# Block-sparse attention and soft mixture of experts: scores of two query blocks in one pass over the array

## The chip, the cores and the metric

The kernel runs on one core of one Trainium2 chip. The core has a matrix engine (TensorE, here PE, whose loads of stationary operands are listed as PEld), VectorE (DVE), ScalarE (ACT), GpSimd (POOL) and a queue engine (SP) that issues transfers. The metric is the device time of one execution in microseconds; the median of the runs counts. All data are float32.

## The reference, cut to what matters

```python
# B, H, S, D = 4, 8, 768, 64; blocks of 32 tokens, 24 blocks
scores = scale * np.matmul(q, k.transpose(0, 1, 3, 2))
mask = np.abs(blk_i - blk_j) <= 1                       # window of three blocks
mask = mask | (blk_i == 0) | (blk_j == 0) | (blk_i == n_blocks - 1) | (blk_j == n_blocks - 1)
for qb in range(n_blocks):
    for kb in sampled_blocks[qb]:                       # three drawn blocks per query block
        mask[qb*32:(qb+1)*32, kb*32:(kb+1)*32] = True
attn = softmax(np.where(mask, scores, -1e9));  x = attn @ v      # x: 3072 tokens, 512 wide
logits = x @ phi                                        # 32 slots: 8 experts, 4 slots each
slot_input = softmax(logits, over tokens).T @ x
slot_out[e] = relu(slot_input[e] @ w1[e]) @ w2[e]       # w1: 512 x 1024, w2: 1024 x 512
out = softmax(logits, over slots) @ slot_out
```

So the first and the last query block see all 768 keys ("dense"), and each of the 22 others sees at most 256: the two global blocks, its window of three, and three drawn blocks.

## The kernel before

**Units.** The attention is a list of 104 units, 26 per batch. A dense unit holds two heads of query blocks 0 and 23; there are four per batch. A sparse unit is one query block i (1 to 22) with all eight heads. Heads are stored in pairs: the transposed keys of a pair lie on 128 partitions, 64 for each head (`ktile`, four pairs of 768 columns, one batch at a time).

**Stages of a sparse unit.** `stage_k` gathers 256 key columns for the four pairs into one of `NKST` buffers `kst`: GpSimd copies the global and the window blocks (lines 190, 193), ScalarE the three drawn ones (line 199), whose numbers it loads into registers. `stage_v` loads the matching rows of V into one of eight buffers `vst`: SP issues the global and window rows, GpSimd an indirect gather of 96 rows (line 219). `do_qk` computes scores with four matmuls (line 306): the stationary operand holds, for one pair of heads, 64 columns, two heads of 32 queries, and each head's column is zero on the other head's 64 partitions; the 256 staged keys are the moving operand. Pairs 0 and 2 write partitions 0 to 63 and pairs 1 and 3 partitions 64 to 127 of one PSUM tile `s` of 128 by 2 by 256. `do_soft` takes the row maximum on VectorE (`nm`, line 322) and the exponential on ScalarE (`p`, line 325). `do_tr` transposes the 128 by 512 probabilities in four pieces on PE (`ps`, line 354) and copies them to SBUF (`ptt`), one unit on ScalarE (line 335), the next on VectorE (line 337). Four units make a tile of 128 tokens; `av_half` then multiplies by V for heads 0 to 3 and for heads 4 to 7 (`av`, line 391, 32 matmuls each), V's last column being ones for the sum, and VectorE divides (lines 398 to 400).

**Stages of a dense unit.** The same steps under the names `sd` (line 298), `nm`, `pd`, `psd` (line 345, six transposes in two banks), `ptd` and `avd` (line 371).

**Behind each tile** run the steps of `moe_front`: transposes of the tokens (`mxt`), logits (`mlp`, `mlt`), their running maximum and exponential (`nmx`, `dT`), a transpose (`md`) and the sum into the slot input (`ms`, `sacc`). `EOFF` says how many half steps after the tile each comes.

**Order.** PE and VectorE execute in the order in which the code is written: the loop at line 585 calls, for unit n, the scores of unit n+2 (line 589), what is due first (`X1`), the transposes of unit n, and what is due second (`X2`). ScalarE, GpSimd and SP get their order from a scheduler. SP issues nearly all transfers in one queue: queries (`qc`, three buffers), V, keys of the next batch, and pieces of the expert weights, `NPRE` of which are loaded during the attention.

**PSUM** has eight banks: the tag "s" (`SB` of them, scores), "pt" (`TB`, everything transposed or of `moe_front`) and "av" (two). A tile of a tag waits until the tile that last used that bank has been read.

**The experts** follow: `pf` (line 714) and `pso` (line 722) read each weight once, with 32-column stationary operands on four column strips, and `po` (line 814) combines.

Of the kernel before, what the change touches and what calls it, by code (L numbers as in the profile page):

```python
# [11 lines left out]
F32 = mybir.dt.float32  # L12
# [9 lines left out]
P = 128  # L22
# [3 lines left out]
NE, SE, FF = 8, 4, 1024  # L26
NT = S // P
# [17 lines left out]
# experts: w2 in CS column parts, weights in pieces of WP, NPRE of them loaded during the attention  # L45
# [7 lines left out]
NPRE, NLA, NLB = 29, 3, 12  # L53
# [9 lines left out]
def attn_moe_kernel(ctx, tc, qT, kT, vtab, sampled, phi, w1, w2, out):  # L63
# [9 lines left out]
    # the weights come in pieces of [P, WP]  # L73
# [75 lines left out]
    # ================= attention =================  # L149
# [7 lines left out]
    # but for the first, in the order in which the end of the attention frees them, the last first  # L157
# [3 lines left out]
    qc = [pst.tile([P, NP, 2, 2 * BLK], F32, name=f"qc{n}") for n in range(NQ)]  # L161
# [7 lines left out]
    def load_q(b, c):  # L169
        SP.dma_start(out=qc[(b * (NB // 2) + c) % NQ], in_=qT[b, c])  # L170

    def q_of(b, i):
        c = (i + 1) // 2
        return qc[(b * (NB // 2) + c) % NQ][:, :, (i + 1) % 2, :]
# [60 lines left out]

    class U:
        pass

    # the tokens go in tiles of four blocks: (1, 2, 0, 23), (3 .. 6), ... (19 .. 22)
# [26 lines left out]
    def do_stage(u):  # L266
        if u.dense:
            if u.pair == 0 and u.b:
                load_q(u.b, 0)
                load_k(u.b)  # L270
                load_q(u.b, 1)
# [634 lines left out]
```

## Time and profile before

| | us |
|---|---|
| median of 3 runs | 395.05 (394.22 to 395.6) |
| span of the profiled execution, first to last instruction | 410.4 |
| attention within it, about | 13 to 347 |
| PE busy | 353.6 |
| DVE, ACT, POOL busy | 220.0, 209.9, 142.3 |

The profiled execution has no other time than its span, which is 15.4 us above the median; its rows are used for durations and shares. Its mean granted clock of PE is 0.963. Several rows of a product stand for one matmul: a float32 matmul makes two records, a transpose one. A group of the profile is written `line engine operation out<-in shapes xcount | busy us, mean ns of one | idle before it, and what ended that idle time`.

### The profile page before, as it was taken

The numbers are of one execution on the slowest core, as the hardware profiler recorded it, in microseconds if no ns is written. First come the engines' busy times: TensorE is split into PE (matmuls) and PEld (weight loads), VectorE is DVE, ScalarE is ACT, GpSimd is POOL, SyncE is SP. The second block draws the span as 40 slices with busy tenths as digits, with TensorE's granted clock in tenths as the row PEclk, the third lists the DMA queues.
The fourth block names the chain that finished last, engine by engine and source line by source line (L and its number), as shares of the span: only waits on it lengthen the run. The fifth ranks groups of instructions, "written<-read, shape, count | busy, mean of one in ns | idle before, by whom it ended". The sixth has DMA issues, their size and how long they took to land.

```text
span 410.4 us, 14102 instructions
## 1 busy us (share of the span) xinstructions
PE 353.6 (86%) x5525; PEld 228.1 (56%) x5525; DVE 220.0 (54%) x618; ACT 209.9 (51%) x689; POOL 142.3 (35%) x216
## 2 busy tenths in 40 slices
PE   5788988799899867998999698989989899799970
PEld 2456655467566544665665465657556556435550
DVE  3655635466455535676565356756556687501350
ACT  1655756466457625672766276638556563310350
POOL 1625425432153544234445244333453243120000
PEclk9999999899899989999999799999999899999995
DMA  7977999989859979999599759965965499899978
GB/s 242 299 221 224 312 291 246 287 272 314 214 153 286 264 237 312 292 274 286 140 271 274 244 164 277 309 173 147 265 162 138 124 242 396 308 357 410 360 248 250
DMA packets 47841, 105.56 MB, mean 257 GB/s; under 512 B 6976, under 2 KB 13856, under 8 KB 47776
## 3 DMA queue, kind: packets, MB, share of 16 engines
q1 hardware_dynamic: 42144, 87.08, 68.5%
q0 software_dynamic: 5632, 17.58, 16.4%
q8 instruction: 44, 0.72, 0.8%
q14 instruction: 21, 0.17, 0.1%
HBM read 98.34 MB, written 6.29 MB: 255 GB/s over the span
## 4 chain that ended last, share of the span: by engine, by line
PE 81%; issue 6%; DVE 3%; DMA 3%; SPq 2%; ACT 1%; POOL 1%; ACTq 0%; POOLq 0%; DVEq 0%
PE s L306 22%; PE av L391 13%; PE ps L354 12%; PE sd L298 6%; PE pso L722 4%; PE pf L714 3%; PE mxt L413 3%; PE avd L371 3%; PE psd L345 3%; PE mlt L465 2%; PE ms L497 2%; PE mlp L458 2%; DMA ktile<-in_kT_dram 2%; PE po L814 2%; DMA vst<-in_vtab_dram 1%
## 5 line engine op out<-in xcount | busy, mean ns | idle before, releaser
L219 POOL DMA_INDIRECT vst<-in_vtab_dram,gidx x88 | 83.3, 946 | 111.9 <-PE av L391 89.2
L306 PE MATMUL s<-kst,qc 128*64 128x256 f32 x704 | 100.8, 404 | 8.9 <-issue 6.3
L199 ACT ACTIVATE kst<-ktile 128x128 f32 x264 | 67.0, 312 | 56.7 <-PE ps L354 18.9
L322 DVE TENSOR_REDUCE nm<-s 128x2 f32<-128x512 f32 x88 | 60.4, 687 | 45.5 <-PE s L306 20.4
L325 ACT ACTIVATE p<-s,nm 128x256 f32<-128x256 f32 x176 | 73.9, 475 | 12.0 <-DVE nm L322 9.6
L193 POOL TENSOR_SCALAR kst<-ktile 128x384 f32<-128x384 f32 x88 | 45.3, 519 | 76.0 <-PE s L306 62.2
L391 PE MATMUL av<-vst,ptt 128*32 128x65 f32 x2816 | 59.2, 225 | 12.0 <-issue 10.9
L306 PEld LDWEIGHTS s<-kst,qc 128*64 128x64 f32 x704 | 44.7, 139 | 38.0 <-issue 19.2
L391 PEld LDWEIGHTS av<-vst,ptt 128*32 128x32 f32 x2816 | 49.2, 111 | 20.4 <-issue 17.9
L354 PE MATMUL ps<-ident,p 128*128 128x128 f32 x352 | 58.9, 291 | 0.0
L354 PEld LDWEIGHTS ps<-ident,p 128*128 128x128 f32 x352 | 38.0, 143 | 22.1 <-issue 14.0
L337 DVE COPY ptt<-ps 128x512 f32<-128x512 f32 x44 | 30.2, 685 | 34.2 <-PE av L391 22.0
L335 ACT COPY ptt<-ps 128x512 f32<-128x512 f32 x44 | 25.8, 587 | 40.3 <-PE ps L354 26.2
L319 ACT ACTIVATE pd<-sd,nb 128x384 f32<-128x384 f32 x32 | 17.7, 579 | 32.0 <-DVE nb L316 17.1
L298 PE MATMUL sd<-ktile,qc 128*128 128x384 f32 x64 | 27.9, 564 | 5.1 <-DMA ktile<-in_kT_dram 5.1
L400 DVE TENSOR_TENSOR x<-av,rs 128x256 f32<-128x256 f32 (+1 forms) x48 | 20.3, 423 | 1.6
L313 DVE TENSOR_REDUCE nm<-sd 128x1 f32<-128x384 f32 x32 | 17.1, 553 | 7.2 <-PE sd L298 4.8
L337 DVE COPY xT<-mxt 128x512 f32<-128x512 f32 (+2 forms) x25 | 16.5, 661 | 7.4 <-PE mxt L413 3.5
L345 PE MATMUL psd<-ident,pd 128*128 128x128 f32 x96 | 14.8, 293 | 5.3 <-DVE ptt L337 5.3
L298 PEld LDWEIGHTS sd<-ktile,qc 128*128 128x128 f32 x64 | 12.3, 215 | 12.4 <-DMA qc<-in_qT_dram 4.3
L371 PEld LDWEIGHTS avd<-vst,ptd 128*64 128x64 f32 x384 | 13.7, 143 | 7.0 <-DVE ptd L337 2.1
L497 PE MATMUL ms<-x,d 128*32 128x128 f32 x192 | 10.2, 285 | 8.3 <-DVE ptt L337 7.1
(110 smaller groups left out, 352.4 us busy)
## 6 DMA issues: line engine op xcount, KB each, us to landing
w<-in_w_dram SPq DMA_DIRECT2D x64, 512.0 KB
vst<-in_vtab_dram SPq DMA_DIRECT2D x80, 195.0 KB
qc<-in_qT_dram SPq DMA_DIRECT2D x47, 256.0 KB
vst<-in_vtab_dram SPq DMA_DIRECT2D x24, 260.0 KB
ktile<-in_kT_dram SPq DMA_DIRECT2D x15, 384.0 KB
out_dram<-ob SPq DMA_DIRECT2D x20, 256.0 KB
vst<-in_vtab_dram SPq DMA_DIRECT2D x72, 65.0 KB
vst<-in_vtab_dram,gidx POOLq DMA_INDIRECT x88
```

What stands on the lines that cost most here:

```text
L193: POOL.tensor_scalar(out=st[:, :, BLK:P], in0=kv[:, :, (i - 1) * BLK:(i + 2) * BLK], scalar1=SCALE, scalar2=1.0, op0=ALU.mult, op1=ALU.mult)
L199: ACT.activation(out=st[:, :, 160 + BLK * j:192 + BLK * j], in_=kv[:, :, ds(vals[j] * BLK, BLK)], func=AF.Copy, scale=SCALE)
L219: POOL.indirect_dma_start(out=st[32:128, 1, :], out_offset=None, in_=vflat, in_offset=bass.IndirectOffsetOnAxis(ap=gidx[:, b, i:i + 1], ax ...
L298: PE.matmul(u.s[n], lhsT=qc[u.b * (NB // 2) % NQ][:, u.pair].rearrange("p a c -> p (a c)"), rhs=ktile[:, u.pair, 384 * n:384 * (n + 1)], s ...
L306: PE.matmul(u.s[64 * c:64 * c + 64, hf, :], lhsT=q[:, p, :], rhs=u.kst[:, p, :], start=True, stop=True)
L322: DVE.tensor_reduce(out=nm, in_=u.s, axis=AX.X, op=ALU.max, negate=True)
L325: ACT.activation(out=u.p[:, hf, :], in_=u.s[:, hf, :], func=AF.Exp, bias=nm[:, hf:hf + 1], scale=1.0)
L337: DVE.tensor_copy(out=out, in_=in_)
L345: PE.transpose(ps[:, k, :], u.p[g][:, k * P:(k + 1) * P], ident)
L354: PE.transpose(ps[:, 2 * hf + k, :], u.p[:, hf, k * P:(k + 1) * P], ident)
L371: PE.matmul(a[64 * h2:64 * h2 + 64, u.pair, :], lhsT=u.pt[k][:, 64 * h2:64 * h2 + 64], rhs=vd[u.b][k][:, h * 65:h * 65 + 65], start=(k == ...
L391: PE.matmul(a[32 * c:32 * c + 32, hh, :], lhsT=u.pt[:, 2 * hf + k, hh * 32:hh * 32 + 32], rhs=u.vst[:, k, h * 65:h * 65 + 65], start=(k == ...
```

## The change

One score pass now serves two query blocks, a "pair" of units with blocks 2g+1 and 2g+2. Heads are paired as (p, p+4): the first four heads lie on partitions 0 to 63, the last four on 64 to 127. A score matmul takes one head of one block: a stationary operand of 64 partitions by 32 columns, without zeros, and the 64 partitions of `kst` that hold this head. Head p of the first four goes to partitions 32p of one PSUM tile, head p+4 to the same partitions of a second tile. So unit r of a pair no longer holds one block with eight heads but both blocks with four heads; its tile is again 128 by 2 by 256, the middle index being the block. Maximum, exponential, transposes and copies keep their sizes and their count. `av_half` for heads 4r to 4r+3 now follows unit r of the tile's second pair. It has 32 matmuls as before.

With it change: query transfers (`qT` without zeros, 128 KB per pair; the dense blocks' zero-padded queries apart, `qd`, 256 KB per batch), `NKST` 3 to 4, `SB` 3 to 4, `TB` 3 to 2, `NPRE` 29 to 28, the order of a batch's first units, the last of `EOFF`, and the end of the last tile. Comments were removed too; they are left out here.

```diff
+NG2 = NB // 2 - 1
-NKST, NV, NQ = 3, 8, 3
+NKST, NV, NQ = 4, 8, 3
-SB, TB = 3, 3
+SB, TB = 4, 2
-ORDER0 = "DDSDDSS"
-ORDER = "DSDDDSS"
+ORDER0 = "DDSSDDSS"
+ORDER = "DSSDDDSS"
-EOFF = [3, 6, 8, 9, 11, 15]
+EOFF = [3, 6, 8, 9, 11, 14]
-NPRE, NLA, NLB = 29, 3, 12
+NPRE, NLA, NLB = 28, 3, 12
...
-    qc = [pst.tile([P, NP, 2, 2 * BLK], F32, name=f"qc{n}") for n in range(NQ)]
+    qd = pst.tile([P, NP, P], F32, name="qd")
+    qc = [pst.tile([P, NP, 2, BLK], F32, name=f"qc{n}") for n in range(NQ)]
...
-        for i in range(1, NB - 1):
-            u = U()
-            u.b, u.i, u.dense = b, i, False
-            sparse.append(u)
+        for g in range(NG2):
+            us = [U(), U()]
+            for r, u in enumerate(us):
+                u.b, u.g, u.r, u.dense, u.pair_of = b, g, r, False, us
+                u.i = 2 * g + 1 + r
+            sparse += us
...
-        if u.i % 2 == 0 and u.i // 2 + 1 < NB // 2:
-            load_q(u.b, u.i // 2 + 1)
+        if u.r == 1 and u.g + 1 < NG2:
+            load_q(u.b, u.g + 1)
         u.kst = stage_k(u.b, u.i)
...
-        else:
-            q = q_of(u.b, u.i)
-            u.s = psA.tile([P, 2, 256], F32, tag="s", name="s", bufs=SB)
-            for hf in range(2):
-                for c in range(2):
-                    p = 2 * hf + c
-                    PE.matmul(u.s[64 * c:64 * c + 64, hf, :], lhsT=q[:, p, :],
-                              rhs=u.kst[:, p, :], start=True, stop=True)
+        elif u.r == 0:
+            q = qc[(u.b * NG2 + u.g) % NQ]
+            for v in u.pair_of:
+                v.s = psA.tile([P, 2, 256], F32, tag="s", name="s", bufs=SB)
+            for j in range(2):
+                kst_ = u.pair_of[j].kst
+                for p in range(NP):
+                    for r in range(2):
+                        s_ = slice(64 * r, 64 * r + 64)
+                        PE.matmul(u.pair_of[r].s[32 * p:32 * p + 32, j, :], lhsT=q[s_, p, j, :],
+                                  rhs=kst_[s_, p, :], start=True, stop=True)
...
             for k in range(2):
                 for u in us:
-                    c = quad(u.i)
-                    PE.matmul(a[32 * c:32 * c + 32, hh, :], lhsT=u.pt[:, 2 * hf + k, hh * 32:hh * 32 + 32],
-                              rhs=u.vst[:, k, h * 65:h * 65 + 65], start=(k == 0), stop=(k == 1))
+                    for j in range(2):
+                        c = quad(2 * u.g + 1 + j)
+                        PE.matmul(a[32 * c:32 * c + 32, hh, :], lhsT=u.pt[:, 2 * j + k, hh * 32:hh * 32 + 32],
+                                  rhs=u.pair_of[j].vst[:, k, h * 65:h * 65 + 65], start=(k == 0), stop=(k == 1))
...
-                t = (u.i + 1) // 4
-                bytile.setdefault((u.b, t), []).append(u)
-                if u.i % 4 == 2:
-                    us = bytile.pop((u.b, t))
+                t = (u.g + 1) // 2
+                bytile.setdefault((u.b, t, u.r), []).append(u)
+                if u.g % 2 == 0:
+                    us = bytile.pop((u.b, t, u.r))
+                    go = lambda b=u.b, t=t, us=us, hf=u.r: av_half(b, t, us, hf)
                     if n == N - 1:
-                        last = [lambda hf=hf, us=us: av_half(B - 1, NT - 1, us, hf) for hf in range(2)]
+                        last = go
                     else:
-                        for hf, X in ((0, X1), (1, X2)):
-                            X.setdefault(n + 1, []).append(lambda b=u.b, t=t, us=us, hf=hf: av_half(b, t, us, hf))
+                        X1.setdefault(n + 1, []).append(go)
...
-    last[0]()
-    one()
     one()
     e = moe_front(B - 1, NT - 1)
-    last[1]()
+    last()
+    one()
...
-    kt = k.reshape(B, NP, 2, S, D).transpose(0, 1, 2, 4, 3).reshape(B, NP, 2 * D, S)
+    kt = k.reshape(B, 2, NP, S, D).transpose(0, 2, 1, 4, 3).reshape(B, NP, 2 * D, S)
```

How the order on the engines moves. First PE in the middle of a batch, between two groups of av matmuls (rows: line, operation, out<-in, size of the output, count). Before:

```order
L306 MATMUL s<-kst_91,qc_102 64x256 x4
L354 MATMUL ps<-ident,p 128x128 x4
L482 MATMUL md<-ident,dT 128x32
L413 MATMUL mxt<-ident,x 128x128 x4
L306 MATMUL s<-kst_100,qc_103 64x256 x4
L354 MATMUL ps<-ident,p 128x128 x4
L306 MATMUL s<-kst_101,qc_103 64x256 x4
L458 MATMUL mlp<-xT,phis 32x128 x4
L354 MATMUL ps<-ident,p 128x128 x4
L497 MATMUL ms<-x,d 32x128 x4
```

And now:

```order
L359 MATMUL ps<-ident,p 128x128 x8
L489 MATMUL md<-ident,dT 128x32
L420 MATMUL mxt<-ident,x 128x128 x4
L311 MATMUL s<-kst_91,qc_104 32x256 x8
L311 MATMUL s<-kst_100,qc_104 32x256 x8
L359 MATMUL ps<-ident,p 128x128 x4
L504 MATMUL ms<-x,d 32x128 x4
L465 MATMUL mlp<-xT,phis 32x128 x4
```

The transposes of two units now stand next to each other with md and mxt behind them, all in the "pt" banks; ms stands ahead of mlp. VectorE at the same place, now, from the copy of the first of those two units on:

```order
L342 COPY ptt<-ps 128x512
L327 TENSOR_REDUCE nm<-s 128x2
L342 COPY d<-md 128x32
L493 SCALAR_TENSOR_TENSOR ssum<-ssum,al,sm 128x1
L342 COPY xT<-mxt 128x512
L327 TENSOR_REDUCE nm<-s 128x2
L342 COPY ptt<-ps 128x512
L327 TENSOR_REDUCE nm<-s 128x2
L507 SCALAR_TENSOR_TENSOR sacc<-sacc,al,ms 128x128
```

The copy of the third transposed unit stands behind the reduction of scores that PE computes just ahead of that unit's transposes, as it did before. In the dense units (PE), before:

```order
L345 MATMUL psd<-ident,pd 128x128 x6
L497 MATMUL ms<-x,d 32x128 x4
L306 MATMUL s<-kst_91,qc_104 64x256 x4
L465 MATMUL mlt<-lp,sel_69 128x128
L466 MATMUL mlt<-sel_69,lp 128x32
L371 MATMUL avd<-vst_94,ptd 64x65 x4
```

And now:

```order
L376 MATMUL avd<-vst_94,ptd 64x65 x4
L350 MATMUL psd<-ident,pd 128x128 x6
L376 MATMUL avd<-vst_99,ptd 64x65 x4
L376 MATMUL avd<-vst_95,ptd 64x65 x4
L376 MATMUL avd<-vst_94,ptd 64x65 x4
L350 MATMUL psd<-ident,pd 128x128 x6
```

One of the four groups of transposes psd has no score product between it and the avd that uses it.

More of the change, by code (lines that the diff above doesn't have):

```diff
@@ L62, in attn_moe_kernel @@
 @with_exitstack
-def attn_moe_kernel(ctx, tc, qT, kT, vtab, sampled, phi, w1, w2, out):
+def attn_moe_kernel(ctx, tc, qD, qT, kT, vtab, sampled, phi, w1, w2, out):
     nc = tc.nc
@@ L167, in load_k, with load_q @@
             SP.dma_start(out=ktile[:, p, :], in_=kT[b, p])
[L169 to L174, printed above, removed]
+    def load_q(b, g):
+        SP.dma_start(out=qc[(b * NG2 + g) % NQ], in_=qT[b, g])
     nsp = [0]
@@ L268, in do_stage @@
             if u.pair == 0 and u.b:
+                SP.dma_start(out=qd, in_=qD[u.b])
+                load_k(u.b)
                 load_q(u.b, 0)
[L270 to L271 removed]
             return
[L273 to L274 removed]
+        if u.r == 1 and u.g + 1 < NG2:
+            load_q(u.b, u.g + 1)
         u.kst = stage_k(u.b, u.i)
@@ L297, in do_qk @@
             for n in range(2):
-                PE.matmul(u.s[n], lhsT=qc[u.b * (NB // 2) % NQ][:, u.pair].rearrange("p a c -> p (a c)"),
-                          rhs=ktile[:, u.pair, 384 * n:384 * (n + 1)], start=True, stop=True)
-        else:
-            q = q_of(u.b, u.i)
-            u.s = psA.tile([P, 2, 256], F32, tag="s", name="s", bufs=SB)
-            for hf in range(2):
-                for c in range(2):
-                    p = 2 * hf + c
-                    PE.matmul(u.s[64 * c:64 * c + 64, hf, :], lhsT=q[:, p, :],
-                              rhs=u.kst[:, p, :], start=True, stop=True)
+                PE.matmul(u.s[n], lhsT=qd[:, u.pair], rhs=ktile[:, u.pair, 384 * n:384 * (n + 1)], start=True, stop=True)
+        elif u.r == 0:
[9 more added lines that the diff above has]
+                                  rhs=kst_[s_, p, :], start=True, stop=True)
     def do_soft(u):
@@ L369, in av_dense @@
             for h2 in range(2):
-                h = 2 * u.pair + h2
+                h = u.pair + 4 * h2
                 PE.matmul(a[64 * h2:64 * h2 + 64, u.pair, :], lhsT=u.pt[k][:, 64 * h2:64 * h2 + 64],
```

32 lines of the change are left out of this document (16 added, 16 removed).

## The prediction

> **What bounds the kernel now.** I read the page first, then the chain of waits, then the table by stretches.
>
> ```profile
> span 410.4 us, 14102 instructions
> PE 353.6 (86%) x5525; PEld 228.1 (56%) x5525; DVE 220.0 (54%) x618; ACT 209.9 (51%) x689; POOL 142.3 (35%) x216
> PE 81%; issue 6%; DVE 3%; DMA 3%; SPq 2%; ACT 1%; POOL 1%; ACTq 0%; POOLq 0%; DVEq 0%
> ```
>
> TensorE (PE) carries 81% of the chain that ends last. The attention lasts from about 13 to 347 us. The rows of the table by stretches, for all of it and for two groups of four sparse units (a tile of tokens), give busy time of PE, PEld, DVE, ACT, POOL, then the granted clock, DMA share and GB/s:
>
> ```profile
> 13.00:347.00 334.00, 300.08 (x4978) 199.74 (x4978) 196.55 (x544) 191.24 (x645) 133.73 (x190) 0.97 0.85 244
> 129.75:142.11 12.36, 10.91 (x205) 7.19 (x209) 6.87 (x19) 7.19 (x26) 5.78 (x9) 1.00 1.00 285
> 297.84:310.00 12.16, 10.73 (x206) 7.04 (x209) 6.87 (x19) 6.99 (x26) 5.79 (x9) 1.00 0.68 175
> ```
>
> PE is busy in 300 of 334 us. The two tiles take nearly the same time although the DMA share is 1.00 in one and 0.68 in the other, so transfers do not set the pace. The chain through the second tile, in order of time (start, length, what):
>
> ```profile
> 297.84 1.17 PE av L391 x64
> 299.01 0.59 PE ps L354 x4
> 299.60 1.04 PE av L391 x64
> 300.65 1.01 PE s L306 x8
> 301.66 0.59 PE ps L354 x4
> 302.25 0.18 PE md L482
> 302.43 0.59 PE mxt L413 x4
> 303.01 1.01 PE s L306 x8
> 304.03 0.59 PE ps L354 x4
> 304.61 1.01 PE s L306 x8
> 305.63 0.35 PE mlp L458 x8
> 305.98 0.65 PE ps L354 x4
> ...
> 306.65 0.69 DVE nm L322
> 307.35 0.61 DVE ptt L337
> ...
> 308.00 0.43 PE ms L497 x8
> 308.42 1.01 PE s L306 x8
> ```
>
> Two things are to be seen. Scores (s) are four pieces of 1.01 us, a third of the tile. And between 306.63 and 308.00 PE waits 1.37 us: ms needs a bank of the "pt" rotation that the copy ptt empties, and that copy stands behind a reduction in VectorE's (DVE's) order. This is the only stall of the tile.
>
> **The scores: what is saved.** A unit's four matmuls are eight records (two passes each) in 1.01 us; 88 units make 88.9 us. What is a record worth? These pieces of the chain are a full-width product of 384 columns, and second-layer expert products of 256 columns on quarters of the array:
>
> ```profile
> 99.17 1.49 PE sd L298 x4
> 374.85 6.61 PE pso L722 x120
> ```
>
> A full-width record takes 1.49/4 = 0.372 us, scaled to 256 columns 0.248. A score record now takes 1.01/8 = 0.126, so a group of two (both column halves) lasts 0.253. An expert record takes 6.61/120 = 0.055, a group of four (all column quarters) 0.220. So a group lasts 0.22 to 0.25 us whatever the number of column strips that share it. The new pair of units has 16 matmuls, 32 records, in four groups of eight (four strips, two row halves). No row of the trace has two row halves at work together; I bound it. If all eight run together: 4 x 0.253 = 1.01 us (4 x 0.220 = 0.88 at best). If the row halves follow each other: 8 x 0.253 = 2.02. I take 1.01, since strips in the other direction share with no loss in the rows above, and the two halves write different banks. Saved: 44 pairs x (2.02 - 1.01) = 44.4 us; bounds 50 and 0. The other arithmetic is unchanged: as many reductions, exponentials, transposes and av matmuls.
>
> The Trainium skill, "TensorE: Matmul & The Clock Gate", Part 3, section "Measured speedup vs the span model", speaks against full sharing: four row tiles gave 3.07x and nine tiles 6.32x. An estimate from that page for eight tiles is 5.6x. On the 0.497 us that a 256-column matmul takes alone (two records of 0.248) 16 matmuls would then take 1.42 us a pair, and the saving would be 26 us. The trace disagrees for columns: four strips give 0.248/0.055 = 4.5x.
>
> **What is given back: the banks.** The "pt" rotation (ps, psd, mxt, mlp, mlt, md, ms) falls from three banks to two, because two units' scores now need two banks at once. What frees a bank:
>
> ```profile
> L322 DVE TENSOR_REDUCE nm<-s 128x2 f32<-128x512 f32 x88 | 60.4, 687 | 45.5 <-PE s L306 20.4 <-PE ps L354 18.4 <-ACT p L325 2.8
> L337 DVE COPY ptt<-ps 128x512 f32<-128x512 f32 x44 | 30.2, 685 | 34.2 <-PE av L391 22.0 <-PE sd L298 10.1 <-PE ps L354 1.3
> L335 ACT COPY ptt<-ps 128x512 f32<-128x512 f32 x44 | 25.8, 587 | 40.3 <-PE ps L354 26.2 <-PE s L306 8.4 <-issue 5.6
> L400 DVE TENSOR_TENSOR x<-av,rs 128x256 f32<-128x256 f32 x40 | 17.0, 424 | 1.3
> L199 ACT ACTIVATE kst<-ktile 128x128 f32 x264 | 67.0, 312 | 56.7 <-PE ps L354 18.9 <-issue 13.0 <-PE s L306 11.8
> ```
>
> In the new order PE does av, ps, ps, md, mxt, s (two units), ps, ms, mlp. Let av end at 0. The ps end at 0.59 and 1.18. DVE first does what av released (the multiplication alone 0.42, two small operations before it, together about 0.75), then the copy of the first ps, 0.685: md, which takes that bank, starts at 1.48 instead of 1.18, 0.30 late. mxt needs ScalarE's (ACT's) copy of the second ps, 1.18 + 0.04 + 0.587 = 1.81, against 1.66 at which md ends: 0.15 late; ACT has up to six key copies (0.312 each, overlapping) ahead of such a copy in its order, and I add 0.2. The scores then end at 3.6, the third ps 0.59 later; its copy stands behind the reduction of those scores: 3.6 + 0.04 + 0.69 + 0.685 = 5.0, while mlp, which takes that bank, would start at 3.6 + 0.59 + 0.43 = 4.6: 0.4 late. Together about 1.1 us per tile, 24.2 us for 22 tiles. Bounds: nothing, if the copies are early, and 2 us per tile, if ACT's are twice as late as worked out. Against that stands what the trace already pays, in the waits of PE:
>
> ```profile
> PE av L391 <- issue: 10.9, 8, 3.3
> PE ms L497 <- DVE ptt L337: 7.1, 5, 1.9
> PE s L306 <- issue: 6.3, 4, 2.5
> ```
>
> The 7.1 us go: ms now takes mxt's bank, emptied during the scores. Net +17.1.
>
> **Smaller terms.** In the dense units each group of six transposes psd had a score product (1.01) behind it before avd; now once per batch avd follows at once and waits for both copies, about 0.6 us, 4 x 0.6 = +2.5 (bounds 0 and 5). PE's instruction records grow from 2 x 5525 by 2 x 704, 13%; if the "issue" stalls in front of av and s (10.9 + 6.3) are late instructions, they grow by 13%: +2.3 (0 to 5). Then transfers:
>
> ```profile
> 350.00:372.00 22.00, 20.54 (x205) 8.91 (x209) 5.99 (x28) 4.44 (x12) 4.04 (x7) 1.00 0.90 339
> w<-in_w_dram SPq DMA_DIRECT2D x64, 512.0 KB
> qc<-in_qT_dram SPq DMA_DIRECT2D x47, 256.0 KB
> ```
>
> One weight piece of 512 KB less is loaded ahead; at 339 GB/s that is +1.5 us in the expert stage, where the DMA share is 0.90 (nothing, if PE there hides it). Queries fall from 47 issues of 256 KB to 44 of 128 KB and four of 256 KB; they are issued ahead on SP's queue and hidden by PE work, so I count 0, and the lower traffic covers the shorter stage. Without that cover, 0.85 x 334 = 284 us of DMA work would still fit into the new 313. The fourth key stage lets ACT and GpSimd run further ahead, which both halves of the pair need: 0.
>
> Sum: -44.4 + 17.1 + 2.5 + 2.3 + 1.5 = -21.0. The profiled span would go from 410.4 to 389.4. The profiled execution is 15 us above the median of 395.05; I take the difference over unchanged: **374 us**.
>
> **Rivals.** (1) The waits do not come: copies are early enough, the 7.1 goes and the small terms stay: -44.4 - 7.1 + 6.3 = -45, 350 us. For it: DVE is busy in 6.87 of 12.16 us; against it: the order on DVE, by which the third copy cannot precede the reduction. (2) Half of the sharing is lost: 1.5 us per pair, saved 22.9, given back 23.4: 395 us, no change. For it: the bound between 1.01 and 2.02 is open; against it: column strips lose nothing. The page named above would land near here. (3) The change does not do what it says: row halves follow each other, a pair costs 1.76 to 2.02 (8 x 0.220 or 0.253), 0 to 11 us saved, 23.4 given back: 407 to 418 us, slower. (4) The two banks decide: every transposed block waits for a copy queued behind others on DVE or ACT; from 2.0 us per tile on, 22 tiles eat the 44 us; at 2.4 us it is -44.4 + 52.8 - 7.1 + 6.3 = +7.6, 403 us. For it: the one stall that the tile shows is of this kind and is already 1.37 us with three banks; against it: my chain gives half.
>
> **How the numbers follow.** Chances: forecast 0.60 (its own range 363 to 385, by 0.6 to 1.6 us of waits per tile), rival 1 0.12, rival 2 0.10, rival 3 0.10, rival 4 0.08. A measurement can tell about 0.3% from no change. Faster by more: 0.60 + 0.12 + 0.04 of rival 2 = 0.76; within: 0.04; slower: 0.10 + 0.08 + 0.02 = 0.20. The range from 355 to 402 leaves out rival 3 and part of rivals 1 and 4, under 0.2.
>
> **What would show it.** In the changed profile the score line should show 1408 records, and a pair in the chain 0.9 to 1.1 us for 32 records; 1.8 or more means rival 3, about 1.5 rival 2. In a tile, md, mxt and mlp should follow waits for ptt of 0.2 to 0.5 us each, and ms none. A tile as free of other stalls as the quoted one should take 12.16 - 2.02 - 1.37 + 1.1 = 9.9 us. The forecast is wrong if waits of PE for ptt sum to over 45 us, or if the pair is not near 1 us.

## The result: 5% slower, and the profile after

The changed kernel takes 413.3 us (median), the kernel before, beside it on the same chip, 394.6 us. The ratio is 1.053, with an interval from 1.045 to 1.061. The forecast was 374 us, the stated range 355 to 402. Ratios leave out executions over 1.5% longer than the fastest of the same kernel, here and below, so they can differ by up to about 1% from those of the medians beside them.

The page of the changed kernel has these rows for the span, the busy times and the chain of waits:

```profile
span 410.8 us, 15471 instructions
PE 322.8 (79%) x6229; PEld 215.3 (52%) x6229; DVE 222.6 (54%) x618; ACT 212.8 (52%) x689; POOL 141.9 (35%) x220
PE 52%; DVE 13%; ACT 11%; DMA 11%; issue 6%; ACTq 2%; SPq 1%; DVEq 0%
```

PE carried 81% of the chain before; now it carries 52%, and VectorE (DVE), ScalarE (ACT) and transfers carry 35%. The group of scores, before and now (busy, mean of one, idle before it and who ended it):

```profile
L306 PE MATMUL s<-kst,qc 128*64 128x256 f32 x704 | 100.8, 404 | 8.9 <-issue 6.3
L311 PE MATMUL s<-kst,qc 64*32 64x256 f32 x1408 | 55.0, 413 | 6.4 <-ACT kst L198 2.9
```

The scores fell from 100.8 to 55.0 us of PE, so what the change is about came in full: 45.8 us. What came with it is seen best in one tile. First a tile of the kernel before (stretch, length, busy time of PE, PEld, DVE, ACT, POOL, clock, DMA share, GB/s), then the tile at the same place in the change and a second tile of the change, with a few more records:

```profile
292.11:302.42 10.31, 10.31 (x196) 6.89 (x195) 6.28 (x16) 7.42 (x28) 3.71 (x7) 1.00 0.61 160
```

```profile
295.83:306.43 10.60, 8.81 (x226) 6.17 (x226) 6.57 (x17) 8.14 (x29) 4.72 (x7) 1.00 0.62 175
223.29:234.31 11.02, 9.01 (x234) 6.42 (x234) 6.92 (x18) 7.70 (x28) 5.75 (x9) 1.00 0.60 163
```

Before, an undisturbed tile was PE work without a gap, 10.31 of 10.31 us. Now PE works 8.81 us of 10.60: 1.5 us of work are gone, and 1.8 us of waiting have taken their place. The chain through the second one, from one mxt to the next (start, length, what):

```profile
223.29 0.66 PE mxt L420 x4
223.94 1.14 PE s L311 x32
225.08 0.67 DVE nm L327
225.75 0.61 DVE ptt L342
226.36 0.04 issue
226.40 0.43 PE mlp L465 x8
226.83 1.31 PE av L398 x64
228.14 0.59 PE ps L359 x4
228.73 1.02 PE s L311 x32
...
231.29 0.29 ACT kst L198
231.59 0.72 ACT p L330 x2
232.31 0.35 ACT dT L480 x2
232.66 0.18 ACT al L484
232.85 0.08 ACT lst L485
232.93 0.04 issue
232.97 0.67 PE ps L359 x4
233.64 0.02 issue
233.67 0.59 ACT ptt L340
234.26 0.04 issue
234.31 0.65 PE mxt L420 x4
```

The pair of scores takes 1.02 to 1.14 us. Three times the chain leaves PE: ahead of mlp for the copy ptt behind the reduction nm (1.3 us), ahead of ps for lst (1.7 us), and ahead of mxt for ScalarE's ptt (0.65 us). PE has a little other work meanwhile and idles 11.02 - 9.01 = 2.0 us of these 3.7. The second is the largest: ps needs the bank that mlt holds until ScalarE has read it for dT and lst, and ScalarE has key copies and two exponentials ahead of these. Over the whole kernel, PE's longest waits are these (total, times, longest); that of the last row lies at the start of the kernel and was there before (5.1 us):

```profile
PE ps L359 <- ACT lst L485: 18.5, 12, 4.9
PE av L398 <- issue: 13.7, 6, 4.3
PE mxt L420 <- ACT ptt L340: 5.8, 12, 0.5
PE mlp L465 <- DVE ptt L342: 5.5, 12, 1.0
PE sd L301 <- DMA ktile<-in_kT_dram: 5.5, 2, 4.3
```

The batch changes got longer as well. The two intervals between tiles around a batch change sum to 31.0, 30.0 and 31.0 us, against 23.6, 23.4 and 24.6 in the kernel before. The chain at the second one, and the table for two stretches there:

```profile
165.00 9.52 DMA ktile<-in_kT_dram
...
177.24 0.08 ACT lst L485
177.32 0.04 issue
177.37 1.13 PE ps L359 x4
```

```profile
165.00:174.60 9.60, 5.75 (x190) 4.22 (x189) 3.94 (x11) 2.43 (x7) 0.22 (x1) 1.00 0.87 256
174.60:180.00 5.40, 2.58 (x13) 1.88 (x12) 2.22 (x7) 4.43 (x19) 4.40 (x9) 0.54 0.87 287
```

The next batch's keys land late, ScalarE's copies of them stand ahead of p, dT, al and lst of the old batch, and PE waits 2.4 us for lst. When it goes on its granted clock is 0.54: four transposes take 1.13 instead of 0.59 us. But the lower clock begins at 175.0, when this wait has just begun. Ahead of it lies another wait, with no cause in the profile (start, length, what, idle before):

```profile
173.73 0.66 PE L398 MATMUL av<-vst,ptt 128*32 128x65 f32 x32 [3.36 <-issue]
```

The Trainium skill ("TensorE: Matmul & The Clock Gate", "What's actually happening") says that the clock falls to half after at least one idle window of about 3.4 us. The trace agrees here, with 3.36 us and 0.54; elsewhere in it half the clock also follows shorter waits (2.7 us, at 89.2).

**The account.** PE outside the scores was busy 353.6 - 100.8 = 252.8 us and is now 322.8 - 55.0 = 267.8: 15.0 us more for the same arithmetic. The clock, 0.963 before and 0.917 now, makes 252.8 x 0.963 / 0.917 = 265.5 of it, that is 12.7 of the 15.0 us. The span outside PE's busy time is 410.8 - 322.8 = 88.0 us. For the kernel before it would be about 394.6 - 1.8 - 353.6 = 39.2 us, an estimate, since its profiled execution was longer than the timed ones; it takes PE's busy time to be the same in both. So -45.8 (scores) + 15.0 (slower PE) + 48.8 (waits) = +18.0.

### The profile page after: what moved, and what is told of

It is laid out like the page before. It is cut to its first block, busy times and chain, and to the rows that moved or that the text cites. A ratio compares the mean times of both kernels' runs of the same rounds, so it can differ in the third digit from the quotient of the medians.

```text
span 410.8 us, 15471 instructions
## 1 busy us (share of the span) xinstructions
PE 322.8 (79%) x6229; PEld 215.3 (52%) x6229; DVE 222.6 (54%) x618; ACT 212.8 (52%) x689; POOL 141.9 (35%) x220
## 3 DMA queue, kind: packets, MB, share of 16 engines
q0 software_dynamic: 5632, 17.58, 16.1%
## 4 chain that ended last, share of the span: by engine, by line
PE 52%; DVE 13%; ACT 11%; DMA 11%; issue 6%; ACTq 2%; SPq 1%; DVEq 0%
DMA ktile<-in_kT_dram 10%; PE s L311 9%; PE av L398 8%; PE ps L359 6%; PE sd L301 5%; PE pf L720 4%; DVE ptt L342 4%; PE mxt L420 4%; PE pso L728 4%; DVE nm L327 3%; PE avd L376 3%; ACT kst L198 3%; PE psd L350 3%; ACT ptt L340 2%; ACT p L330 2%
## 5 line engine op out<-in xcount | busy, mean ns | idle before, releaser
L198 ACT ACTIVATE kst<-ktile 128x128 f32 x264 | 63.8, 302 | 46.5 <-DMA ktile<-in_kT_dram 13.7
L330 ACT ACTIVATE p<-s,nm 128x256 f32<-128x256 f32 x176 | 73.3, 471 | 17.4 <-DVE nm L327 16.7
L398 PE MATMUL av<-vst,ptt 128*32 128x65 f32 x2816 | 61.0, 224 | 17.6 <-issue 13.7
L398 PEld LDWEIGHTS av<-vst,ptt 128*32 128x32 f32 x2816 | 52.5, 111 | 24.5 <-issue 16.6
L359 PEld LDWEIGHTS ps<-ident,p 128*128 128x128 f32 x352 | 41.6, 152 | 42.1 <-ACT lst L485 21.4
L311 PE MATMUL s<-kst,qc 64*32 64x256 f32 x1408 | 55.0, 413 | 6.4 <-ACT kst L198 2.9
L311 PEld LDWEIGHTS s<-kst,qc 64*32 64x32 f32 x1408 | 23.1, 112 | 23.2 <-issue 13.2
L301 PE MATMUL sd<-ktile,qd 128*128 128x384 f32 x64 | 28.2, 571 | 5.5 <-DMA ktile<-in_kT_dram 5.5
L405 DVE TENSOR_SCALAR rs<-av 128x4 f32<-128x4 f32 (+1 forms) x48 | 7.6, 159 | 42.2 <-PE av L398 41.7
L420 PE MATMUL mxt<-ident,x 128*128 128x128 f32 x92 | 17.8, 325 | 11.0 <-ACT ptt L340 5.8
L342 DVE COPY xT<-mxt 128x512 f32<-128x512 f32 (+2 forms) x25 | 16.6, 664 | 17.6 <-PE mxt L420 17.2
L301 PEld LDWEIGHTS sd<-ktile,qd 128*128 128x128 f32 x64 | 13.0, 226 | 12.2 <-issue 4.8
L189 POOL TENSOR_SCALAR kst<-ktile 128x256 f32<-128x256 f32 x16 | 6.4, 397 | 37.0 <-DMA ktile<-in_kT_dram 28.6
```

What stands on the lines that cost most here:

```text
L198: ACT.activation(out=st[:, :, 160 + BLK * j:192 + BLK * j], in_=kv[:, :, ds(vals[j] * BLK, BLK)], func=AF.Copy, scale=SCALE)
L301: PE.matmul(u.s[n], lhsT=qd[:, u.pair], rhs=ktile[:, u.pair, 384 * n:384 * (n + 1)], start=True, stop=True)
L311: PE.matmul(u.pair_of[r].s[32 * p:32 * p + 32, j, :], lhsT=q[s_, p, j, :], rhs=kst_[s_, p, :], start=True, stop=True)
L330: ACT.activation(out=u.p[:, hf, :], in_=u.s[:, hf, :], func=AF.Exp, bias=nm[:, hf:hf + 1], scale=1.0)
L342: DVE.tensor_copy(out=out, in_=in_)
L359: PE.transpose(ps[:, 2 * hf + k, :], u.p[:, hf, k * P:(k + 1) * P], ident)
```

## The experiments

They ran in five sets, each on a chip of its own, and the kernel before was timed beside each set. On the third chip it took 391.7 us, much as on the chip of the result; on the other four 414 to 416 us, where all kernels are slower (the last section says how). So only kernels of one set are compared in us, others by their ratio.

| kernel | us | before beside it | ratio (interval) |
|---|---|---|---|
| b0: the kernel before, profiled again | 419.0 | 414.6 | one run |
| one_key_load | 440.0 | 414.6 | 1.068 (1.062 to 1.074) |
| two_key_tiles | 441.1 | 414.6 | 1.070 (1.064 to 1.077) |
| three_banks | 432.9 | 414.6 | 1.048 (1.043 to 1.054) |
| change_again | 446.3 | 413.7 | 1.080 (1.073 to 1.088) |
| before_two_banks | 446.5 | 413.7 | 1.077 (1.068 to 1.086) |
| act_as_written | 432.1 | 413.7 | 1.045 (1.036 to 1.054) |
| two_key_tiles_act_as_written | 434.5 | 413.7 | 1.047 (1.039 to 1.055) |
| scores_twice | 467.7 | 391.7 | 1.193 (1.183 to 1.204) |
| one_av_bank | 403.6 | 391.7 | 1.032 (1.023 to 1.040) |
| one_av_bank_act_as_written | 378.6 | 391.7 | 0.963 (0.952 to 0.973) |
| three_banks_act_as_written | 393.6 | 391.7 | 1.006 (1.001 to 1.011) |
| before_act_as_written | 435.5 | 416.1 | 1.054 (1.037 to 1.070) |
| before_one_av_bank_act_as_written | 449.9 | 416.1 | 1.083 (1.059 to 1.106) |
| dense_first | 446.2 | 416.1 | 1.085 (1.075 to 1.094) |
| one_av_bank_act_as_written_two_key_tiles | 422.4 | 416.1 | 1.026 (1.016 to 1.035) |
| fastest_again | 417.5 | 414.9 | 1.000 (0.995 to 1.005) |
| old_scores_again | 447.6 | 414.9 | 1.068 (two executions, no interval) |

The theories: (1) the keys' reload is exposed by its place in SP's queue; (2) by the single key tile; (3) two banks for what is transposed cost more than the scores save; (4) ScalarE's scheduled order holds PE up.

### The kernel before once more

No edit. 

> The kernel before, profiled again, since its first profiled execution (span 410.4 us) was some 15 us longer than its timed runs. If the difference lay in that one execution's late instructions (PE waited 17.2 us with nothing to wait for in front of av and s), this span is 393 to 397 us, those waits are under 5 us, and tiles take 10.3 to 10.5 us throughout. If the profiler itself costs 15 us on this kernel, the span is about 410 again.

It took 419.0 us with a span of 417.2. This chip is one of the slow kind, so the run did not give the undisturbed trace it was meant for. The waits without a visible cause were as in the first profile (16.1 us in front of av and s, 17.2 there); they are not an accident of one execution.

### The keys

```diff
-        for p in range(NP):
-            SP.dma_start(out=ktile[:, p, :], in_=kT[b, p])
+        SP.dma_start(out=ktile, in_=kT[b].rearrange("p d s -> d p s"))
```

> The change, with the next batch's keys loaded by one transfer of 1.5 MB in place of four, so that SP cannot put five loads of V between the first part and the other three (in the changed kernel's trace these go out 3.6 us apart: part 1 at 160.5, parts 2 to 4 at 164.06). Theory 1 (the keys' reload is exposed because of its place on SP's queue): each of three batch changes gets about 3.5 us shorter, 402 us. Theory 2 (it is exposed because there is one key tile, and the place does not matter): no change, 411 to 414 us. Theory 3 (banks and ScalarE's order alone made the change slow): no change either.

```diff
-    ktile = pk.tile([P, NP, S], F32, name="ktile")
+    ktiles = [pk.tile([P, NP, S], F32, name=f"ktile{n}") for n in range(2)]
...
-NPRE, NLA, NLB = 28, 3, 12
+NPRE, NLA, NLB = 25, 3, 12
```

> The change, with two key tiles in turn instead of one, and 25 weight pieces loaded ahead instead of 28 (three pieces of 512 KB are worth at most 4.6 us in the expert stage at its 339 GB/s). The two tile-to-tile intervals around a batch change sum to 31.0, 30.0 and 31.0 us in the changed kernel, and to 23.6, 23.4 and 24.6 in the kernel before. Theories 1 and 2 (the exposed reload is what made the change slower): 20 us less, 390 to 398 us, and no wait of PE, ScalarE or GpSimd for keys over 1 us in all but the first batch. Theory 3: under 6 us less, 407 us or more.

Ratios 1.068 and 1.070, where the change has 1.080 on a like chip (change_again): about 5 us each, not 10 and 20. The intervals touch that of the change, so even these 5 us are not clear of the noise, and in two_key_tiles the three weight pieces fewer may hide up to 4.6 us of gain (estimate in the expectation). The edit did what it should: in its trace no engine waits for the keys of a later batch, where in the trace of the result ScalarE does so for 13.7 us and GpSimd for 28.6. Yet the intervals around the three batch changes sum to 89.9 us, against 99.2 in change_again and 73.9 in b0. Theories 1 and 2 fall as the main cause; what makes the batch changes long is seen next.

### The banks, alone and in the change

```diff
-SB, TB = 4, 2
+SB, TB = 3, 3
```

> The change, with three banks for scores and three for what is transposed, instead of four and two. Theory 3 (two banks eat what the scores save): the waits of PE for ptt and lst, 36.2 us in the changed kernel, fall below 15 us, a tile goes from 10.6 to 11.2 us to about 9.9, and the time falls by 15 to 20 us to 393 to 398. Theories 1 and 2: the tiles may gain, but the batch changes stay at 30 to 31 us a pair of intervals, and the time does not get under 400 us. If scores then wait for p with three banks (the pair needs a bank that the exponential just before has to free), the wait only changes its name: no change, 410 to 415 us.

Ratio 1.048 against 1.080: 13 us better. PE's waits at ps for lst are gone (md has 3.9), but with three score banks scores and av now wait (av for ptt 19.1 us, s for pd 6.7). The six intervals around the batch changes sum to 86.9 us instead of 99.2, 12 of the 13 us gained. So theory 3 is half right here, and the test is blunt: PSUM has no room for 4, 3 and 2 banks.

> The changed kernel itself, to be timed and profiled beside the next three. On the chip of the last runs the kernel before took 414.6 us instead of 394.6 and PE's signals came up to 3 us late, so those runs are to be set against this one. If this chip delays all kernels alike, the ratio to the kernel before is 1.04 to 1.06 again. If the three variants of the last runs were in truth no faster than the change, it is 1.05 or less on that chip.

The change itself has 1.080 on such a chip instead of 1.053. So the first three variants were each a little faster than it, three_banks clearly.

In the kernel before:

```diff
-SB, TB = 3, 3
+SB, TB = 4, 2
```

> The kernel before with the change's banks alone: four for scores, two for what is transposed (three and three before). Theory 3 (two banks cost about 1.1 us per tile or more): 20 to 45 us slower, ratio 1.05 to 1.11, with PE's waits for ptt, lst and lp at 30 us or more. If the old order of PE, with a score product between any two users of a bank, hides them: ratio 1.00 to 1.02, and the waits in the change belong to its order, not to the banks.

446.5 against 413.7 us: the bank split alone costs the old kernel 32.8 us, as much as the whole change (446.3). Its waits of PE:

```profile
PE mxt L413 <- DVE ptt L337: 11.0, 3, 3.7
PE ps L354 <- DVE ptt L337: 9.9, 9, 1.5
...
PE mxt L413 <- ACT ptt L335: 5.3, 7, 2.4
```

The old order, with a score product between most users of a bank, does not hide them. The 11.0 us in front of mxt are three waits of 3.7 us, one at each batch change, where the dense units' transposes use the same two banks: the six intervals there grow from 73.9 us (b0) to 93.0, 19 of the 32.8 us.

Theory 3 holds as one cause, not as the only one. With the same banks the old and the new kernel take the same time, although the new one has 45.8 us less of scores. So on such a chip the change gives back about 78 us (45.8 + 32.6, an estimate), and about 46 of them come on top of what the bank split costs the old kernel: with PE's new order, ScalarE's, the fourth key stage and the smaller edits. Of these only ScalarE's order was undone by itself.

### ScalarE's order

`MAN` lists the engines that keep the order of the code during the attention; `TMAN`, for a later part, stays the same set.

```diff
-MAN = {mybir.EngineType.PE, mybir.EngineType.DVE}
-TMAN = MAN | {mybir.EngineType.Activation}
+MAN = {mybir.EngineType.PE, mybir.EngineType.DVE, mybir.EngineType.Activation}
+TMAN = MAN
```

> The change, with ScalarE in the order in which the code is written, as PE and VectorE are: the three key copies of unit n+5 stand ahead of the exponential of unit n+2, so no six of them stand ahead of p, dT, al and lst. Theory 4 (ScalarE's scheduled order, not the number of banks, holds PE up at lst): the 18.5 us that PE waits at ps for lst fall under 6, and the time falls by 8 to 15 us. Theory 3: the waits move to ptt and the time stays within 4 us. Theories 1 and 2: at the three batch changes the next batch's key copies now stand ahead of exponentials and the time grows by up to 15 us.

432.1 against 446.3 us in the same set, 14 us, in the range of theory 4. The trace says where:

```profile
PE mlp L465 <- DVE ptt L342: 13.0, 12, 1.1
...
PE ps L359 <- ACT lst L485: 1.7, 3, 0.9
```

The wait for lst fell from 16.0 us (change_again) to 1.7; the wait for VectorE's ptt stayed, 13.0 us after 16.7.

> Both: two key tiles (25 weight pieces ahead) and ScalarE as written. If the change's loss is the exposed reload and ScalarE's order together, this is the kernel that gains: batch changes 24 to 26 us a pair of intervals, tiles 10 to 10.4 us, 22 to 30 us less than the change, ratio to the kernel before 0.97 to 1.00. If it is as slow as the change, the loss lies elsewhere: in the order of PE itself.

434.5 us: the second key tile adds nothing to ScalarE's order. The loss is not keys and ScalarE together; the banks remain.

The same edit in the kernel before:

> The kernel before with ScalarE in the order of the code, and nothing else. If the scheduled order of ScalarE hurts only in the change (bursts of six key copies ahead of p, dT, al, lst; in the kernel before three or fewer stood there): within 1% of the kernel before. If it hurts both alike, 10 to 15 us faster, ratio 0.96 to 0.975, and the 14 us that the same edit took off the change say nothing about the change.

Neither: it is about 22 us slower (ratio 1.054). (That three or fewer copies stood there was miscounted: up to five stand directly ahead of the exponentials and dT in the kernel before, six in the change.) Scores then wait for GpSimd's part of the key stage:

```profile
PE s L306 <- POOL kst L190: 7.7, 3, 3.5
```

So the scheduled order served the old kernel and hurts the new one.

### The scores

```diff
-                    for r in range(2):
+                    for r in (0, 1, 0, 1):
```

> The change, with each score matmul issued twice in a row (same result): 64 records per pair instead of 32, PE's score work back at 2.02 us a pair, 44 pairs, 44 us more PE work. Theory 3, sharpened by the last runs (with two banks PE waits for copies, and score work only fills those waits; the kernel before with two banks was as slow as the change): the time grows by 5 to 20 us over the change. If PE's work sets the time, it grows by 40 to 45 us. Less than 5 us would mean that the halved scores were worth nothing at all here.

467.7 us, where the change would take about 391.7 x 1.053 = 412.5. My sharpened theory, that scores only fill waits, is refuted. Page and group of this kernel:

```profile
span 468.8 us, 18299 instructions
L311 PE MATMUL s<-kst,qc 64*32 64x256 f32 x2816 | 112.3, 403 | 12.6 <-issue 9.2 <-ACT kst L198 2.9 <-ACT pd L324 0.5
```

The scores grew by 57.3 us of PE and the span by 58.0 us over that of the change. So score work that is added to the change is paid in full. A reduction follows the scores and a copy follows the reduction, which is why I take it to stand in the chain. It does not follow that score work taken away from the old kernel comes back in full: with two banks the old and the new scores took the same time, in different orders.

### Enough banks

Since avd keeps its bank over a batch's dense units, one av bank needs these first:

```diff
-SB, TB = 4, 2
+SB, TB = 4, 3
-ORDER0 = "DDSSDDSS"
-ORDER = "DSSDDDSS"
+ORDER0 = "DDDDSS"
+ORDER = "DDDDSS"
...
-            dav[u.b] = psA.tile([P, NP, D + 1], F32, tag="av", name="avd")
+            dav[u.b] = psA.tile([P, NP, D + 1], F32, tag="av", name="avd", bufs=1)
...
-        a = psA.tile([P, 4, D + 1], F32, tag="av", name="av")
+        a = psA.tile([P, 4, D + 1], F32, tag="av", name="av", bufs=1)
```

> The change with four banks for scores, three for what is transposed and one, not two, for av. Since avd keeps that bank over a batch's four dense units, all four dense units now stand first in each batch (order DDDDSS). Theory 3: with both rotations whole, the tiles get rid of the waits for ptt and lst at ps, mxt and mlp, and the time falls by 25 to 45 us from the change, to 0.97 to 1.02 of the kernel before. If one av bank makes av wait for the division on VectorE (about 0.8 us, 48 times), 38 us come back and the time is that of the change. If the loss lies elsewhere (order of PE, keys), it stays above 1.06.

Ratio 1.032 instead of 1.053: 9 us, less than the 25 to 45 expected. md now waits for lst (6.8 us), av for ptt (10.0), and av without a visible cause for 26.2.

With ScalarE as written as well:

> The same with ScalarE in the order of the code, which alone took 14 us off the change. Theory 3 and 4 together: 8 to 14 us less than with one av bank alone, ratio to the kernel before 0.94 to 0.99, so the halved scores show at last. If both cures act on the same wait: no more than 4 us less.

378.6 us, ratio 0.963: faster than both kernels, by 13 us than the kernel before. The second cure took 25 us, more than expected. Busy times, a tile, and the waits of PE:

```profile
PE 311.5 (82%) x6229; PEld 215.7 (57%) x6229; DVE 217.2 (58%) x618; ACT 212.4 (56%) x689; POOL 141.7 (38%) x220
```

```profile
268.90:278.40 9.50, 8.58 (x226) 6.35 (x225) 6.48 (x17) 7.74 (x27) 3.92 (x7) 1.00 0.44 117
```

```profile
PE av L398 <- issue: 16.4, 10, 3.9
PE av L398 <- DVE ptt L342: 12.1, 20, 1.5
```

No wait for lst or mlp is left, the tile takes 9.5 us, and PE outside the scores is busy 311.5 - 52.0 = 259.5 us instead of 267.8 (52.0 is its score group). At the three batch changes the intervals sum to 30.5, 23.1 and 24.3 us, with one key tile.

> Three banks for scores and three for what is transposed, and ScalarE in the order of the code. Each took about 13 us off the change by itself. If they act on different waits: 26 us, 420 us, ratio 1.01 to 1.02. If on the same: 430 us, ratio 1.04 to 1.045. In both cases scores wait for exponentials, since a pair needs two banks of three.

393.6 us, ratio 1.006, 0.047 below the change on such a chip; on the slower kind each alone took 0.032 and 0.035 off. So they act in part on different waits: alone they would add up to 0.067, though the comparison goes across the two kinds of chip. It still loses 15 us to the kernel with four score banks.

> Control: the change with the dense units first (order DDDDSS) and nothing else, since the kernels with one av bank needed that order. If the order of the first units is worth nothing, ratio 1.045 to 1.065 as the change; the whole gain of one av bank (403.6 us) is then the third bank. If dense first hides or exposes the keys: 5 to 10 us either way.

1.085 against 1.080 for the change on a like chip: the order of the first units is worth nothing, so the gain of one_av_bank is that of the third bank, less what the one av bank costs.

> The fastest kernel so far with two key tiles (25 weight pieces ahead). Theories 1 and 2 in what is left of them: 4 to 10 us faster, ratio 0.94 to 0.955, with the two intervals around a batch change at 20 to 22 us instead of 23.1 to 30.5. If the reload is hidden once ScalarE's order is right: no change, ratio 0.955 to 0.975.

1.026, where the same with one key tile had 1.000 on a chip of the same kind (next). Two key tiles, with three weight pieces fewer, cost rather than help. In the fastest kernel GpSimd still waits 11.3 us for keys, but nothing is gained by taking this wait away.

### What the halved scores are worth under equal conditions

The kernel before with one av bank, four and three others, dense units first and ScalarE as written:

> The old scores under the conditions of the fastest kernel so far: four banks for scores, three for what is transposed, one for av, dense units first, ScalarE as written. The only difference left to that kernel (378.6 us, ratio 0.963) is the score arrangement and the fourth key stage. If the 44 us of the halved scores are all there once the banks are: this one is 415 to 425 us, ratio 1.06 to 1.08. If the tile with halved scores is no longer set by PE but by the chain through VectorE (its tiles took 9.5 to 10.2 us against 10.3 to 10.5 for clean tiles of the kernel before): 390 to 400 us, ratio 0.99 to 1.02.

Its first run fell on another chip than the fastest kernel, so both were put on one:

> The change with one av bank, three banks for what is transposed, dense units first and ScalarE as written, once more (378.6 us, ratio 0.963, on the chip where the kernel before took 391.7). On a chip where the kernel before takes 414 to 416 us: ratio 1.02 to 1.03 if it loses there what the one with two key tiles lost (1.026), and then the two key tiles are worth nothing; ratio above 1.04 if those helped. On a chip as the first: 0.955 to 0.97 again.

> The old scores under the same conditions, beside it on one chip. If the halved scores are worth as much as between the last two (449.9 and 422.4 us): 20 to 35 us slower than the run beside it. If all 44 us show: 40 us or more. If the earlier difference came from the key tiles: under 15 us.

By the ratios, 1.068 against 1.000, the kernel with the new score arrangement is about 28 us faster than the old one with the same banks and the same order on ScalarE; the first run of the old scores had 1.083, with an interval from 1.059 to 1.106. That is about two thirds of the 44 us. It is not the worth of the halved scores alone: the fourth key stage goes with them, and the shared conditions were found for the new kernel, while ScalarE as written costs the old one 22 us by itself. On this kind of chip the fastest kernel is level with the kernel before (1.000), on the other kind 3.7% faster.

## Why the prediction was wrong, point by point

**The scores: right.** 44.4 us were forecast, the group fell by 45.8; a pair takes 1.02 us, 1408 records. Rivals 2 and 3 fall by the same rows: eight tiles of the array work together almost without loss.

**The step that failed is "What is given back: the banks".** It gave 1.1 us per tile, 24.2 us, and 17.1 net. The mechanism was the forecast one, and that of rival 4 (chance 0.08): a transposed block waits for a copy that stands in an engine's queue. The place and the size were wrong. The forecast chain let PE wait in front of md (0.30), mxt (0.35) and mlp (0.4), about 23 us over 22 tiles, and never in front of ps. The trace has 1.7, 11.0 and 5.5 us in front of these three, 18 in all and less than forecast. The rest came in front of ps, where the kernel before has no wait:

```profile
L354 PE MATMUL ps<-ident,p 128*128 128x128 f32 x352 | 58.9, 291 | 0.0
L359 PE MATMUL ps<-ident,p 128*128 128x128 f32 x352 | 62.1, 306 | 23.7 <-ACT lst L485 18.5
```

The forecast gave ScalarE's place in the order 0.2 us a tile, 4.4 us in all, and only at mxt. The bank of mlt, which ps takes and which ScalarE frees behind key copies and exponentials, was in none of the chain's steps. Three of the twelve waits for lst, 9.9 us, lie at the batch changes, where late keys hold ScalarE up too; the other nine take about 1 us each. Putting ScalarE in order took 14 us with two banks and 25 us with three.

**The same step counted sparse tiles alone.** At a batch change the dense units share the two banks, for which the forecast had 2.5 us in all. The six intervals there grew by 20.4 us, from 71.6 to 92.0. In the old kernel the bank split alone lengthens them by 19 of its 32.8 us (before_two_banks), and a third bank takes 12 us off them (three_banks).

**"The fourth key stage lets ACT and GpSimd run further ahead: 0" failed in its sign, as far as the order shows.** In the order of ScalarE's rows six key copies in a row stand directly ahead of p, dT, al and lst in 13 of 24 tiles; before, it was five once and four or fewer otherwise; as written, three. One such place in the change:

```
L194 TENSOR_LOAD sreg
L198 ACTIVATE kst_91<-ktile 128x4x32
L198 ACTIVATE kst_91<-ktile 128x4x32
L198 ACTIVATE kst_91<-ktile 128x4x32
L194 TENSOR_LOAD sreg
L198 ACTIVATE kst_100<-ktile 128x4x32
L198 ACTIVATE kst_100<-ktile 128x4x32
L198 ACTIVATE kst_100<-ktile 128x4x32
L330 ACTIVATE p<-s,nm 128x256 x2
L480 ACTIVATE dT,sm<-mlt,nmx 128x128
L484 ACTIVATE al<-nmx 128x1
L485 COPY lst<-mlt 128x32
```

That the fourth stage is what lets it is argued, not shown: it was not undone by itself.

**"Transfers do not set the pace": true within a tile, false at a batch change.** Keys land late three times. By the two experiments on the keys this is worth about 5 us, not clear of the noise, and nothing that could be measured once ScalarE is in order.

**A term that was not there: the clock.** 15.0 us more PE time for the same work, of which 12.7 go with the granted clock, 0.963 to 0.917. Between 20 and 350 us the clock stands at half for 51 us, in the kernel before for 20. Three of these stretches (17 us: at 93, 257 and 318 us) begin at waits for lst. The other four (34 us: at 56, 73, 148 and 175 us) begin at waits of 1.7 to 4.3 us in front of av and s for which the profile shows no cause. So a wait can cost twice, once as a wait and once in what follows at half the clock, but at most a third of this term hangs on the banks.

**The small terms.** The "issue" waits in front of av and s are 13.7 + 2.6 = 16.3 us after, 17.2 before: the forecast 2.3 us more did not come there, but the fastest kernel has 16.4 + 7.0. They are fewer and longer, though: 8 instead of 12, the longest 4.3 us instead of 3.3. What they are stays open. ms has no wait for ptt any more, as forecast. The dense units' psd and avd wait 3.0 us for ptd, 2.0 before: 1.0 more where 2.5 were forecast. "A clean tile should take 9.9": the change takes 10.6, the kernel with enough banks and ScalarE as written 9.5.

**The test named in the prediction was too narrow.** "Waits of PE for ptt over 45 us" did not come: they are about 21. The rest came under the names lst, lp, kst and d, and in the clock.

**Still open.** The cures bring back 413 - 379 = 34 of some 63 us that were given back (45.8 + 18). The rest is in the fastest kernel's waits (24 us of issue, 17 for ptt) and was not taken apart further. PE's new order and the fourth key stage were not undone by themselves, so what they cost is open.

## What to carry to other kernels

Before a bank is moved from one rotation to another, list for each user of the smaller rotation which engine frees its bank and what stands ahead of that on the engine's order: the wait is as long as that queue, not as long as the copy. Do it for the rare stretches too: here over half of what the banks cost the old kernel lay at three batch changes. Work saved on the bound engine showed here only when the engines that follow it in the chain were ordered for the new pace; an order found for the old kernel (here ScalarE's) may cost more than the saving. And a wait of PE of some us can be paid again in the clock behind it.

## What the runs showed of the chip

**Two kinds of chip.** On four of five chips of the experiments the kernel before takes 414 to 416 us, on the fifth and on that of the result 392 to 395. On the slow ones PE's signals, by which it tells other engines that a product is done, come late. A stretch of two_key_tiles in order of time (start, length, engine and line, idle before):

```profile
324.12 1.09 PE L311 MATMUL s<-kst,qc 64*32 64x256 f32 x32
...
327.20 0.71 ACT L198 ACTIVATE kst<-ktile 128x128 f32 x3 [2.98 <-PE ps L359]
327.26 0.98 POOL L192 TENSOR_SCALAR kst<-ktile 128x384 f32<-128x384 f32 x2 [1.25 <-PE ps L359]
327.28 0.69 DVE L327 TENSOR_REDUCE nm<-s 128x2 f32<-128x512 f32 x1 [2.37 <-remote]
327.32 0.35 SPq L173 DMA_DIRECT2D qc<-in_qT_dram  x1
```

The scores end at 325.21, and four engines that wait for them or for PE's next work go on together at 327.2 to 327.3. In that trace about 47 of 128 signals of scores come over 0.3 us after the end of their matmul, the latest 2.9 us, and 615 of PE's signals are recorded of 659; in the trace of the result it is 1 of 129, and none is missing. The first profile of the kernel before is of the slow kind too (25 of 88 late, 582 recorded of 607), which fits its 15 us above the median. The change loses more there, 8.0% instead of 5.3%, and the fastest kernel is level instead of 3.7% faster; that this is because their chains cross engines more often is not shown. The cause is not known. The Trainium skill ("NOTIFIC — the notification-queue block", "7.1 Overflow: three behaviours, one of which stalls the engine") names a way in which the recording itself can hold an engine up; no run here shows whether it is that.

**Eight tiles share the array almost fully.** Sixteen matmuls of 64 x 32 by 256 columns, 32 records, take 1.02 us: four groups of eight in 0.255 us each, nearly as long as one full-width record of 256 columns (0.248, an estimate scaled from the 384 columns of sd). If each took as long alone as a full-width matmul, the sixteen would take 16 x 0.497 = 7.95 us one after another, so the gain is about 7.8. The Trainium skill ("TensorE: Matmul & The Clock Gate", "Measured speedup vs the span model") has 3.07 for four row tiles and 6.32 for nine tiles in both directions, of other shapes; here the measurement is better than that.
